# Moving most of one attention into the gaps of a recurrent loop, on one Trainium2 core

## The chip, the core and the metric

The kernel runs on one core of one Trainium2 chip. The metric is device time in microseconds (us), the median over several executions of the same program; lower is better. The names of the engines are those of the profile: PE is the matrix engine, PEld its weight loads (they overlap with PE: in the kernel before PE was busy for 1098.6 us and PEld for 645.9 of a span of 1339.3), DVE the vector engine, ACT the scalar engine (it does the exponentials), POOL the general engine, SP the engine that issues the DMA transfers. "PEclk" is the share of full speed that the profile records as granted to PE; in the records it is 1.0 or 0.5 at any time, and 0.5 is called half clock here.

## The reference

Two attentions read the same `x` (2048 tokens of 512 features), and a gate mixes their results.

```python
def _A_ref(x, mem0, Wq, Wk, Wv, Wo, seg_len):     # 32 heads of 128; seg_len 32
    mem = mem0                                    # 8 memory tokens
    for s in range(64):
        h = concat([mem, x[:, 32*s:32*s+32]])     # 40 tokens
        q, k, v = h @ Wq, h @ Wk, h @ Wv
        p = softmax(mask(q @ k.T * scale))        # causal, memory always seen
        o = (p @ v) @ Wo
        mem = o[:, :8]                            # feeds segment s+1
        outs.append(o[:, 8:])

def _B_ref(x, wq, wk, wv, wo, beta):              # 32 heads of 16
    M = z = 0
    for s in range(4):                            # 4 chunks of 512 tokens
        p = softmax(causal(qs @ ks.T * scale))
        a_mem = (phi(qs) @ M) / (phi(qs) @ z + 1e-6)
        o = g * a_mem + (1 - g) * (p @ vs)        # g = sigmoid(beta)
        M += phi(ks).T @ vs;  z += phi(ks).sum()  # phi(t) = t+1 if t>0 else exp(t)
    return o_all @ wo

g = sigmoid((x * gate_w).sum(-1))
return g * a + (1 - g) * b
```

A is a chain: segment s+1 cannot start before the memory rows of segment s are out of `Wo`. B has no such chain between its 32 heads and, apart from the small `M`, none between its chunks. B is therefore work that may be placed nearly anywhere.

## The kernel before

The kernel is a list of operations per engine, in program order; a helper derives the semaphores. First all of B is done, and its result before `wo` stays on the chip (`oT`). Then comes the loop over the 64 segments of A.

B works on four heads at a time ("g"), and in waves of four 128x128 score blocks. One wave is sixteen matmuls and four exponentials of up to 128x512:

```python
        def f_lg(pe):
            ins = None
            for j in range(4):
                for slot, n in enumerate(wv):
                    qc, kc = blocks[n]
                    ins = pe.matmul(pb[j][:, 128 * slot:128 * (slot + 1)],
                                    KTg[32 * j:32 * j + DH, 128 * kc:128 * kc + 128],
                                    QTg[32 * j:32 * j + DH, 128 * qc:128 * qc + 128],
                                    start=True, stop=True, tile_position=(32 * j, 0))
            return ins
        # ... cut ...
        for j in range(4):
            P.op("act", (lambda j=j: (lambda a: a.activation(
                ptb[:, j, 128 * n0:128 * (n0 + len(wv))], pb[j][:, 0:128 * len(wv)], ACT.Exp, scale=SCALE_B)))(),
                 reads=[rbank[j]], writes=[rpts[j]], name="ex%d_%d_%d_%d" % (sb, g, w, j))
```

A segment of A has 40 tokens at most, of which 32 go through the main path (8 memory rows and 24 tokens; the last 8 tokens of four segments are done together as "left" units). A projection puts 32 rows of tokens into one of four column groups of PE, so that four matmuls with 128x32 weights fill a bank ("column-tiled" below). The order of a segment is written out:

```python
        nat_pass("K", 0, "act")
        nat_pass("K", 1, "dve")
        nat_pass("Q", 0, "act")
        tr("K", 0, "dve")
        nat_pass("Q", 1, "act")
        tr("K", 1, "dve")
        tr("Q", 0, "act")
        nat_pass("V", 0, "dve")
        tr("Q", 1, "act")
        scores(0)
        nat_pass("V", 1, "dve")
        sums(0)
        norm(0)
        scores(1)
        take_fill(2)
        # ... cut: sums(1), pv(0), evictions, norm(1), pv(1), evictions ...
        wo(0)
        take_fill(1)
        wo(1)
        aw = aW_sb
        raw = Rs("aWsb")
        evac("dve", aw[:, :], pb[wb["bk"]][:, 0:128], [wb["bk"]], [raw], "aW%d" % s)
        # ... cut ...
        P.op("pe", lambda pe: pe.transpose(pb16[bk][:, 0:128], aw[:, :], ident[:, :]), reads=[raw, Rs("ident")],
             writes=[rbank[bk]], name="aT%d" % s)
        # ... cut: two copies by DVE, one of them into hT, the input of the next segment ...
```

The output projection uses 128 matmuls of 128 columns for each segment: the column group j of PE computes the output columns 128j to 128j+127, for all heads. One eviction and one transposition then give the memory rows for the next segment (the "carry").

```python
                    for h in range(16 * b + 8 * half, 16 * b + 8 * half + 8):
                        for j in range(4):
                            ins = pe.matmul(pb[bk][SEG * j:SEG * (j + 1), 0:128], OT_sb[:, h, 0:SEG],
                                            Wo_sb[:, h, 128 * j:128 * (j + 1)], start=(h == 0), stop=(h == H - 1))
```

The softmax here doesn't subtract the row's maximum and nothing guards it: scores larger than these inputs give would overflow.

## Time and profile before

The median was 1338.86 us in three runs.

In this document "ahead" is the time from the start of the span to the first K projection of segment 0, and "loop" is the rest. Both come from the profiled execution. In the kernel before, the line is drawn at 352.3 us, though this projection starts at 354.0; by the exact definition its loop is 985.3 us. Busy time counts the time in which at least one instruction of the engine runs. Matmuls overlap in the trace: the 8192 of the output projection below last 221 ns each, which would be 1810 us in sum, and keep PE busy for 142.7 us. Busy time therefore does not say how near PE is to its peak.

| before | ahead | loop |
|---|---|---|
| length, us | 352.3 | 987.0 |
| PE busy, us | 231.9 | 866.7 |
| ACT busy, us | 204.5 | 417.2 |
| mean PEclk | 0.78 | 0.99 |
| time at half clock, us (counted from the clock records of the trace) | 152.6 | 27.9 |

From the page of the kernel before, these are the busy time of PE, and PE's busy tenths and granted clock in 40 equal slices of the span.

```profile
PE 1098.6 (82%) x31189; PEld 645.9 (48%) x31237; DVE 600.9 (45%) x1556; ACT 621.8 (46%) x1408; POOL 173.7 (13%) x399
...
PE   4767667675788888888889888898988888988897
...
PEclk8978787667899999999999999999999999999999
```

The first ten slices (335 us, B) have digits of 4 to 7 with a clock of 0.6 to 0.9; the loop has 8 and 9 with a clock near 1. The same kernel by two stretches, where the columns are the stretch, its length, the busy time and the count of instructions of PE, PEld, DVE, ACT and POOL, then PEclk, the share of the DMA engines and GB/s:

```profile
0.00:352.00 352.00, 231.87 (x4732) 153.63 (x4765) 199.27 (x552) 204.54 (x452) 101.52 (x194) 0.78 0.17 62
352.00:1339.00 987.00, 866.73 (x26460) 492.25 (x26473) 401.65 (x1004) 417.22 (x957) 72.20 (x205) 0.99 0.02 6
```

No engine is full ahead of the loop. In the loop PE is busy for 867 of 987 us, and 120 us of it are gaps. Two groups of the page, B's exponentials and the output projection of A, show the duration of one instruction and what the engine waited for just before it:

```profile
L643 ACT ACTIVATE PT_g<-ps 128x512 bf16<-128x512 f32 (+1 forms) x384 | 170.2, 529 | 60.2 <-PE ps L634 57.8
L1099 PE MATMUL ps<-Wo_sb,OT_sb 128*32 128x128 bf16 x8192 | 142.7, 221 | 29.5 <-issue 29.5
```

This view is of PE's own waits in the loop, with the sum, the number and the longest one in us:

```profile
PE ps L1063 <- DVE Pn_sb L1051: 44.9, 60, 1.4
PE ps L1099 <- issue: 29.5, 28, 1.8
PE ps L941 <- DVE hT L1154: 17.5, 14, 1.3
PE ps L854 <- DVE hT L1154: 5.0, 19, 0.3
```

PE waits 44.9 us for normalised probabilities, 22.5 us for the carry (`hT`), and 29.5 us inside the output projection for nothing that the profile shows ("issue"). One such gap in the order of time, with start and duration in us:

```profile
700.73 0.90 PE L1099 MATMUL ps<-Wo_sb,OT_sb 128*32 128x128 bf16 x52
703.29 0.35 PE L1099 MATMUL ps<-Wo_sb,OT_sb 128*32 128x128 bf16 x12 [1.67 <-issue]
```

The run of 128 matmuls stops after 116 of them, and goes on 1.67 us later.

### The profile page before, as it was taken

To read this page: it belongs to the slowest core of one execution; us is meant where nothing else is said; L and a number is where in the kernel's file an instruction comes from. 1 tells how busy PE (TensorE), PEld (TensorE's weight loads), DVE (VectorE), ACT (ScalarE), POOL (GpSimd) and SP (SyncE) were. 2 spreads that over 40 slices of the span, in tenths; PEclk is the share of its full clock that TensorE was granted. 3 is DMA by queue.
4 is the path that set the end of the run, shared out by engine and by line. 5 is a ranking of instruction groups with operands and counts; after the bars stand their busy time and mean duration, and the time that the engine had idled before them with its cause. 6 is when DMAs were issued, how large, how long until landed. Compare 5 with 4: busy or idle time off the path is not lost.

```text
span 1339.3 us, 67341 instructions
## 1 busy us (share of the span) xinstructions
PE 1098.6 (82%) x31189; PEld 645.9 (48%) x31237; DVE 600.9 (45%) x1556; ACT 621.8 (46%) x1408; POOL 173.7 (13%) x399
## 2 busy tenths in 40 slices
PE   4767667675788888888889888898988888988897
PEld 3444445344344545444544445554554545545454
DVE  3556667655333434344443434433443444434343
ACT  3757646475244444444444344434444444434343
POOL 5322312132000000000000000010000000000000
PEclk8978787667899999999999999999999999999999
DMA  9400000000300000000000000000000000000000
GB/s 357 149 2 3 2 2 2 2 2 2 127 4 3 8 8 4 7 4 7 4 8 4 7 3 8 7 4 8 4 7 4 8 4 7 4 7 7 4 4 11
DMA packets 12864, 27.38 MB, mean 20 GB/s; under 512 B 800, under 2 KB 11048, under 8 KB 11048
## 3 DMA queue, kind: packets, MB, share of 16 engines
q1 hardware_dynamic: 12584, 23.09, 4.7%
q8 instruction: 244, 4.00, 1.2%
q14 instruction: 36, 0.29, 0.1%
HBM read 20.99 MB, written 2.10 MB: 17 GB/s over the span
## 4 chain that ended last, share of the span: by engine, by line
PE 68%; DVE 13%; ACT 10%; issue 7%; DMA 2%; SPq 0%; DVEq 0%; POOL 0%; ACTq 0%
PE ps L854 33%; PE ps L1099 10%; ACT PT_g L643 6%; PE ps L863 6%; PE ps L553 2%; PE ps L1063 2%; PE ps L634 2%; PE ps L1019 2%; DVE Pn_sb L1049 1%; PE ps L1039 1%; PE ps L1072 1%; PE ps L923 1%; DVE QTg L557 1%; PE ps L958 1%; DVE V_sb L846 1%
## 5 line engine op out<-in xcount | busy, mean ns | idle before, releaser
L643 ACT ACTIVATE PT_g<-ps 128x512 bf16<-128x512 f32 (+1 forms) x384 | 170.2, 529 | 60.2 <-PE ps L634 57.8
L1099 PE MATMUL ps<-Wo_sb,OT_sb 128*32 128x128 bf16 x8192 | 142.7, 221 | 29.5 <-issue 29.5
L1099 PEld LDWEIGHTS ps<-Wo_sb,OT_sb 128*32 128x32 bf16 x8192 | 123.1, 97 | 45.0 <-issue 35.2
L1139 POOL COPY OTL<-OT_sb 128x256 bf16<-128x256 bf16 x64 | 25.6, 401 | 895.4 <-DVE OT_sb L846 895.4
L846 DVE CAST V_sb<-ps 128x512 bf16<-128x512 f32 x128 | 88.5, 692 | 110.0 <-PE ps L854 110.0
L854 PE MATMUL ps<-Wk_sb,hT 128*32 128x512 bf16 x2048 | 131.3, 400 | 6.3 <-DVE hT L1154 5.0
L854 PE MATMUL ps<-Wq_sb,hT 128*32 128x512 bf16 x2048 | 135.8, 384 | 0.0
L854 PE MATMUL ps<-Wv_sb,hT 128*32 128x512 bf16 x2048 | 134.8, 381 | 0.0
L844 ACT ACTIVATE QN_sb<-ps 128x512 bf16<-128x512 f32 x128 | 76.4, 597 | 124.4 <-PE ps L854 124.4
L844 ACT ACTIVATE KN_sb<-ps 128x512 bf16<-128x512 f32 x64 | 38.2, 597 | 170.0 <-PE ps L854 170.0
L649 POOL TENSOR_SCALAR_AFFINE_SELECT PT_g<-PT_g 128x512 bf16<-128x512 bf16 x128 | 82.5, 645 | 219.6 <-ACT PT_g L643 217.4
L846 DVE CAST KN_sb<-ps 128x512 bf16<-128x512 f32 x64 | 44.3, 692 | 140.7 <-PE ps L854 140.7
L844 ACT ACTIVATE QT_sb<-ps 128x512 bf16<-128x512 bf16 x128 | 76.4, 597 | 45.4 <-PE ps L863 45.4
L846 DVE COPY KT_sb<-ps 128x512 bf16<-128x512 bf16 x128 | 54.4, 425 | 89.2 <-PE ps L863 89.2
L846 DVE CAST OT_sb<-ps 128x320 bf16<-128x320 f32 x128 | 62.8, 490 | 65.7 <-PE ps L1072 64.5
L634 PE MATMUL ps<-QTg,KTg 16*128 16x128 bf16 x1280 | 43.4, 246 | 52.0 <-ACT PT_g L643 48.8
L854 PEld LDWEIGHTS ps<-Wk_sb,hT 128*32 128x32 bf16 x2048 | 55.0, 100 | 63.7 <-DVE hT L1154 17.4
L844 ACT ACTIVATE OT_sb<-ps 128x320 bf16<-128x320 f32 x128 | 54.8, 428 | 47.2 <-PE ps L1072 47.2
L854 PEld LDWEIGHTS ps<-Wq_sb,hT 128*32 128x32 bf16 x2048 | 51.3, 98 | 49.9 <-issue 5.0
L1063 PE MATMUL ps<-Pn_sb,V_sb 32*128 32x40 bf16 x2048 | 35.6, 177 | 47.3 <-DVE Pn_sb L1051 44.9
L854 PEld LDWEIGHTS ps<-Wv_sb,hT 128*32 128x32 bf16 x2048 | 49.5, 95 | 30.5
L846 DVE CAST aW_sb<-ps 128x128 bf16<-128x128 f32 x64 | 18.7, 292 | 97.7 <-PE ps L1099 97.7
(135 smaller groups left out, 1808.2 us busy)
## 6 DMA issues: line engine op xcount, KB each, us to landing
Wk_sb<-in_A_Wk_dram SPq DMA_DIRECT2D x4, 1024.0 KB, 11.5
Wq_sb<-in_A_Wq_dram SPq DMA_DIRECT2D x4, 1024.0 KB, 20.5
Wo_sb<-in_A_Wo_dram SPq DMA_DIRECT2D x4, 1024.0 KB, 19.7
Wv_sb<-in_A_Wv_dram SPq DMA_DIRECT2D x4, 1024.0 KB, 9.2
x_sb<-in_A_x_dram SPq DMA_DIRECT2D x4, 512.0 KB, 5.7
out_dram<-fin_sb SPq DMA_DIRECT2D x16, 128.0 KB, 1.7
wqN_sb<-in_B_wq_dram SPq DMA_DIRECT2D x1, 512.0 KB, 7.4
wkN_sb<-in_B_wk_dram SPq DMA_DIRECT2D x1, 512.0 KB, 8.4
```

The costliest lines, as they stand in the source:

```text
L553: ins = pe.matmul(pb[7][:, 0:LB], wqB_sb[:, c, g * 128:(g + 1) * 128], xT[:, c, T0p:T0p + LB], start=(c == 0), stop=(c == C - 1))
L634: ins = pe.matmul(pb[j][:, 128 * slot:128 * (slot + 1)], KTg[32 * j:32 * j + DH, 128 * kc:128 * kc + 128], QTg[32 * j:32 * j + DH, 128 * q ...
L643: P.op("act", (lambda j=j: (lambda a: a.activation(ptb[:, j, 128 * n0:128 * (n0 + len(wv))], pb[j][:, 0:128 * len(wv)], ACT.Exp, scale=SCA ...
L649: P.op("gp", (lambda n=n: (lambda gq: gq.affine_select(ptb[:, :, 128 * n:128 * (n + 1)], ptb[:, :, 128 * n:128 * (n + 1)], [[0, 4], [1, 128]],
L844: P.op("act", lambda a: a.activation(dst, src, ACT.Copy), reads=[rbank[k] for k in bks], writes=dres, name=name)
L846: P.op("dve", lambda d: d.tensor_copy(dst, src), reads=[rbank[k] for k in bks], writes=dres, name=name)
L854: ins = pe.matmul(pb[bk][SEG * j:SEG * (j + 1), :], lhs(c), w_sb[:, c, n0:n0 + 512], start=(c == 0), stop=(c == C - 1))
L863: ins = pe.transpose(pb16[bk][:, i * 128:(i + 1) * 128], nat[:, b, i * 128:(i + 1) * 128], ident[:, :])
L1019: ins = pe.matmul(pb[bk][SEG * j:SEG * (j + 1), L * i:L * (i + 1)], KT_sb[:, 4 * b + i, j, :], QT_sb[:, 4 * b + i, j, :], start=False, sto ...
L1063: ins = pe.matmul(pb[bks[j]][:, L * i:L * (i + 1)], V_sb[SEG * j:SEG * (j + 1), b, i * E:(i + 1) * E], Pn_sb[SEG * j:SEG * (j + 1), b, L * ...
L1099: ins = pe.matmul(pb[bk][SEG * j:SEG * (j + 1), 0:128], OT_sb[:, h, 0:SEG], Wo_sb[:, h, 128 * j:128 * (j + 1)], start=(h == 0), stop=(h == ...
L1139: P.op("gp", lambda gq: gq.tensor_copy(OTL[par][:, :, 8 * r:8 * r + 8], OT_sb[:, :, SEG:L]), reads=[Rs("OT%d_%d" % (b, hf)) for b in range ...
```

## The change

The intent is to fill PE's gaps in the loop with B's work. B's projections and its first chunk (40 of 160 small "score steps") stay ahead of the loop; their results go to DRAM. The weights of A take 16 MB on the chip (16 loads of 1024 KB on the page); that they leave no room for B's results was the reckoning. The other 120 steps are units inside the first 51 segments, which load what they need from DRAM. At the same time several other things change: how B is computed, the tiling of the output projection, the carry, the order of units within a segment, and the masks and sums of A's softmax, which become four column-tiled matmuls where they were one with 128x128 weights (1,152 more matmuls in all). The whole diff is 1,700 lines long; this is its core.

A step of B is two to four wide matmuls into two banks and one exponential of 128x1024:

```diff
+    def scores(self):                       # one of 160 steps; 10 steps are one job of 8 heads
+        job, G, k = n // 10, (n // 5) % 2, n % 5
+        self.load(job, "k")                 # from DRAM, if not yet there
+        bks = v.BK.pair()
+        # ... cut: which blocks a step has ...
+                    ins = pe.matmul(v.pb[bks[x]][:, o:o + w], KT[e][r, 128 * kc:128 * (kc + 1)], QT[r, q0:q0 + w],
+                                    start=True, stop=True, tile_position=(r.start, 0))
+        P.op("act", lambda a: a.activation(pt[:, :, :], v.ps[:, bks[0]:bks[1] + 1, :], ACT.Exp, scale=v.SCALE_B), ...)
+        # ... cut: causal masks by POOL; pv(), chain() and finish() follow later ...
```

The projections ahead go through `phi`, whose minimum is taken by POOL between an exponential by ACT and a sum by DVE:

```diff
+    def phi(bk, dst, wres, name):
+        P.op("act", lambda a: a.activation(et[:, :], v.pb[bk], ACT.Exp), ...)
+        P.op("gp", lambda g: g.tensor_scalar(et[:, :], et[:, :], 1.0, None, op0=ALU.min), ...)
+        P.op("dve", lambda d: d.scalar_tensor_tensor(dst, v.pb[bk], 0.0, et[:, :], ALU.max, ALU.add), ...)
```

The output projection has 32 matmuls of 512 columns for a segment. Each column group now sums over a quarter of the heads, so four partial sums have to be added. The carry does this: the bank is evicted as a high half (ACT, bf16) and the rest (DVE), and eight matmuls with a selection matrix add and transpose them.

```diff
-                    for h in range(16 * b + 8 * half, 16 * b + 8 * half + 8):
-                        for j in range(4):
-                            ins = pe.matmul(pb[bk][SEG * j:SEG * (j + 1), 0:128], OT_sb[:, h, 0:SEG],
-                                            Wo_sb[:, h, 128 * j:128 * (j + 1)], start=(h == 0), stop=(h == H - 1))
+                for i in range(4):
+                    for j in range(4):
+                        h = 16 * b + 4 * j + i
+                        ins = pe.matmul(pb[bk][SEG * j:SEG * (j + 1), :], OT_sb[:, h, 0:SEG], Wo_sb[:, h, :],
+                                        start=(b == 0 and i == 0), stop=(b == 1 and i == 3))
+                    # ... cut: for two halves of 256 columns, cs ...
+                    evac("act", aW_sb[:, 0, cs], pb[bk][:, cs], [bk], [Rs("aWh%d" % k)], "hi%d_%d" % (s, k))
+                    P.op("dve", lambda d, cs=cs: d.tensor_tensor(aW_sb[:, 1, cs], pb[bk][:, cs], aW_sb[:, 0, cs], ALU.subtract), ...)
+        def w_t():
+                            # ... cut: loops over the four blocks c of columns and k = high, rest ...
+                            ins = pe.matmul(pb[bk][:, SEG * c:SEG * (c + 1)], aW_sb[:, k, 128 * c:128 * (c + 1)], selL[:, :],
+                                            start=(k == 0), stop=(k == 1))
```

The order of a segment is a list (K, Q, V projections; T transpositions; S scores; M sums; N normalisation; PV; E evictions; W output projection; WT carry; Fc and Ff the left units; bS, bP, bT the units of B), with a table of which engine evicts what:

```diff
+A_ORDER = """
+    K1 K0 Q0 Q1 Fc TK0 TQ0 TK1 Ff bP TQ1 bT Fc S0 bS V0 M0 S1 N0 V1 M1 N1 PV0 Fc E0a E0b PV1 W0 E1a E1b W1 Fc bP bP bS
+    WT bS Ff bT""".split()
+A_ENG = dict(K0="dve", K1="act", Q0="act", Q1="act", V0="dve", V1="dve", TK0="dve", TK1="act",
+             TQ0="act", TQ1="act", E0a="act", E0b="act", E1a="act", E1b="dve", last=1)
+    n_pre = DEV.get("n_pre", 40)
+    n_b0, nseg_b = bat.n, DEV.get("nseg_b", 51)
```

## The prediction

> **What bounds the kernel now.** Two phases. By stretches of time, the attention of B, 0 to 337 us: PE about 70% busy, ACT and DVE 60 to 70%, granted PE clock 0.72 to 0.86 for most of it; no engine is full, they wait for each other (PE for ACT's exponentials 44 us, groups by line). The segment loop of A, 347 to 1339 us, 64 segments of 15.5 us: PE busy 868 of 992 us, granted clock 0.98, ACT 417, DVE 402, POOL 72. So B is bound by handovers and A by PE. In the loop PE idles about 124 us: for normalised probabilities (45 us), inside the Wo matmuls with no visible cause ("issue", 29.5 us), for the carried memory at a segment's end (about 25 us).
>
> **What the change does.** B's projections and first chunk (40 of 160 score steps) stay ahead of the loop; 120 steps go into PE's gaps in the first 51 segments.
>
> *Ahead of the loop.* K, Q, V and phi(K): 60 groups of four 128x512 matmuls, about 1.0 us each at the old clock, 60 us. Score steps: 0.25 us of scores (16 matmuls took 0.43 us) and 0.25 us of PV (40 took 1.23 us), 20 us for 40. Exponentials become 128x1024; from 128x256 (0.30 us) and 128x512 (0.52) I estimate 1.0 us, 40 us of ACT, plus 25 us of phi and evictions. PE about 90 us, ACT 65. To this come loads, projections before the first scores, about 20 us of POOL masks ahead of the first causal mask, and the way through DRAM: first steady steps near 28 us. Estimate 125 us in place of 337: minus 210.
>
> *In the loop.* Added PE: 120 x 0.5 = 60 us, chains and transposes 7, the new carry (eight 32-column matmuls for one transpose) 11. Wo goes from 8192 matmuls of 128 columns to 2048 of 512: the same columns, 1.95 us per segment, so streaming gains little (about 6 us), but most of the 29.5 us of issue gaps should go. PE busy: about 935 us. ACT gains 120 x 1.0 and 64 x 0.7 (high halves), to about 590 us; DVE about 490: neither becomes the limit. The carry's chain lengthens by about 1 us, covered by B's steps in 51 segments, not in 13. New waits: a single-buffered K/Q load between jobs, perhaps 15 us in all. Idle: about 85 us. Loop 1020 us, plus 30.
>
> **Sum.** 125 + 1020 = 1145 us. Of 210 us gained ahead, about 30 are given back in the loop. Range 1090 to 1205. Chances: faster by over 2% 0.96, within 2% 0.02, slower 0.02.
>
> [...]filled gaps should keep the loop at 0.98 or more.
>
> **Signs.** Right: the loop begins at 110 to 145 us; a B-carrying segment takes 15.7 to 16.5 us with PE about 92% busy, one without B 14.8 to 15.5; Wo issue gaps below 10 us; exponentials near 1.0 us. Wrong: ACT's long exponentials stand before evictions and softmax on its queue and PE waits for ACT; PE waits for DMA of K/Q or V; the first phase above 160 us because staging waits for stores behind weight loads.
>
> **What would make it wrong.** PE waits on scratch loads in every job (up to 50 us); the carry not covered; or nearly all idle filled (loop below 980).

The sum of this forecast is 125 us ahead and 1020 us in the loop, 1145 us. That filled gaps keep the clock at 0.98 or more was the expectation (1.00 was measured). The figures in it that name no reading of the trace are estimates. Two of them can be set beside the kernel before: about 1.0 us for a group of four 128x512 matmuls, where 32 such groups kept PE busy for 40.6 us (1.27 us each, L553), and 1.95 us of output projection for a segment, where PE was busy for 142.7 us in 64 segments (2.23 us each, L1099).

## More of the kernel before

The weight loads have waits of their own. L863 is the transposition:

```profile
PEld ps L863 <- issue: 27.3, 64, 0.5
PEld ps L863 <- ACT QT_sb L844: 27.2, 64, 0.4
PEld ps L863 <- DVE KT_sb L846: 27.2, 64, 0.4
```

Three times in every segment the load of the identity waits about 0.42 us.

A transposition uses the identity and full 128x128 weights.

## The result

| | before | after |
|---|---|---|
| median, us (range, 4 runs each) | 1338.16 (1333.25 to 1340.42) | 1160.53 (1155.74 to 1162.27) |
| profiled span, us | 1339.3 | 1153.9 |
| ahead, us | 352.3 | 173.9 |
| loop, us | 987.0 | 980.0 |
| PE busy in the loop, us | 866.7 | 898.8 |
| ACT / DVE / POOL busy in the loop, us | 417 / 402 / 72 | 622 / 434 / 162 |
| half clock ahead / in the loop, us | 152.6 / 27.9 | 64.9 / 9.3 |

The ratio was 0.8671, with a 95% interval of 0.8635 to 0.8708, and the result was correct. Every ratio here is the mean time of one kernel's runs over the mean of the other's runs in the same rounds, so it is not quite the ratio of the medians. Executions over 1.5% slower than the fastest of the same kernel are left out of the means.

The kernel is 13% faster. The whole gain is ahead of the loop: the loop took 120 more steps of B and still became 5 to 7 us shorter. These are the same views of the kernel after; first the page.

```profile
PE 1012.0 (88%) x24359; PEld 559.7 (49%) x24389; DVE 491.1 (43%) x1229; ACT 692.1 (60%) x1427; POOL 248.7 (22%) x573
...
PE   4667769999999999999999999999999998988886
...
PEclk8798779999999999999999999999999998999999
```

PE has digits of 9 from the seventh slice (from 173 us) to the segments that have no work of B left. The two stretches:

```profile
0.00:174.00 174.00, 113.19 (x987) 57.68 (x1005) 57.49 (x111) 69.85 (x95) 86.26 (x178) 0.81 0.56 186
174.00:1154.00 980.00, 898.78 (x23380) 502.01 (x23384) 433.62 (x1118) 622.26 (x1332) 162.42 (x395) 1.00 0.06 16
```

The groups that answer to B's exponentials and to the output projection:

```profile
L734 ACT ACTIVATE PTa<-ps 128x1024 bf16<-128x1024 f32 x147 | 150.4, 1024 | 42.2 <-PE ps L726 40.6
...
L1139 PE MATMUL ps<-Wo_sb,OT_sb 128*32 128x512 bf16 x2048 | 126.2, 381 | 0.1
```

The 529 ns of the kernel before are a mean of two shapes: one exponential of 128x512 lasted 602 ns and one of 128x256 384 ns. They overlap with their neighbours, so that ACT was busy for 0.52 us per exponential of 128x512 (131.9 us for 256). One of 128x1024 lasts 1.02 us and keeps ACT busy for about as long, so the wide form saves little: 160 of them take 164 us, where the 384 before took 170.2. The output projection has almost no gaps (0.1 us). PE's waits in the loop:

```profile
PE ps L1102 <- DVE Pn_sb L1092: 25.4, 62, 0.9
PE ps L1160 <- ACT LN_sb L312: 14.8, 31, 0.9
PE ps L1160 <- ACT VL L312: 4.8, 11, 0.9
PE ps L1160 <- DVE aW_sb L1149: 4.7, 4, 1.4
PE ps L987 <- DMA oTg<-scr_oTd: 3.8, 1, 3.8
```

The wait for probabilities fell from 45 to 25 us. The carry (L1160) costs 24.3 us in three lines; the releasers named there are only those that came last by semaphore. DRAM was waited for once for 3.8 us (for a result of B stored just before), and four times, 1.3 us in all, for `QTa`. The part of a segment that had the gap above, in the order of time:

```profile
502.76 2.24 PE L1139 MATMUL ps<-Wo_sb,OT_sb 128*32 128x512 bf16 x32
...
505.36 0.36 PE L772 MATMUL ps<-Va,PTa 128*128 128x17 bf16 x8
505.65 0.39 PE L726 MATMUL ps<-QTa,KTa 32*128 32x512 bf16 x2
506.36 0.58 PE L1160 MATMUL ps<-selL,aW_sb 128*128 128x32 bf16 x8 [0.32 <-ACT LN_sb L312]
```

The 32 matmuls of the output projection run without a gap, then a unit of the left rows, then PV and scores of B stand where PE would wait for the carry's evictions, and only 0.32 us of waiting are left. Finally the weight loads of the transposition (now L885):

```profile
PEld ps L885 <- issue: 28.7, 72, 0.4
```

One such wait per segment is left of three.

### The profile page after: what moved, and what is told of

Same layout as the page of the kernel before. It is cut to its first block, busy times and chain, and to the rows that moved or that the text cites. A ratio compares the mean times of both kernels' runs of the same rounds, so it can differ in the third digit from the quotient of the medians.

```text
span 1153.9 us, 54295 instructions
## 1 busy us (share of the span) xinstructions
PE 1012.0 (88%) x24359; PEld 559.7 (49%) x24389; DVE 491.1 (43%) x1229; ACT 692.1 (60%) x1427; POOL 248.7 (22%) x573
## 3 DMA queue, kind: packets, MB, share of 16 engines
q8 instruction: 192, 3.15, 1.1%
## 5 line engine op out<-in xcount | busy, mean ns | idle before, releaser
L742 POOL TENSOR_SCALAR_AFFINE_SELECT PTa<-PTa 128x256 bf16<-128x256 bf16 (+1 forms) x205 | 90.1, 440 | 419.1 <-ACT PTa L734 387.6
L734 ACT ACTIVATE PTa<-ps 128x1024 bf16<-128x1024 f32 x147 | 150.4, 1024 | 42.2 <-PE ps L726 40.6
L1139 PE MATMUL ps<-Wo_sb,OT_sb 128*32 128x512 bf16 x2048 | 126.2, 381 | 0.1
L1149 DVE TENSOR_TENSOR aW_sb<-ps,aW_sb 128x256 bf16<-128x256 f32 x128 | 48.4, 420 | 128.1 <-ACT aW_sb L312 126.1
L312 ACT ACTIVATE aW_sb<-ps 128x256 bf16<-128x256 f32 x128 | 42.2, 381 | 92.5 <-PE ps L1139 92.5
L1191 POOL COPY OTL<-OT_sb 128x256 bf16<-128x256 bf16 x64 | 25.4, 397 | 319.4 <-DVE OT_sb L314 319.4
L312 ACT ACTIVATE OT_sb<-ps 128x320 bf16<-128x320 f32 x192 | 75.7, 428 | 24.9 <-PE ps L1111 24.9
L726 PE MATMUL ps<-QTa,KTa 32*128 32x512 bf16 (+1 forms) x448 | 55.6, 305 | 24.4 <-DMA QTa<-scr_qTd 13.1
L314 DVE CAST KN_sb<-ps 128x512 bf16<-128x512 f32 x64 | 44.2, 690 | 75.6 <-PE ps L876 75.6
L314 DVE COPY KT_sb<-ps 128x512 bf16<-128x512 bf16 x64 | 27.2, 425 | 111.0 <-PE ps L885 111.0
L1139 PEld LDWEIGHTS ps<-Wo_sb,OT_sb 128*32 128x32 bf16 x2048 | 46.6, 95 | 49.9 <-ACT OT_sb L312 20.7
L1081 ACT ACTIVATE R_sb<-ps 128x160 f32<-128x160 f32 x128 | 38.8, 303 | 33.7 <-PE ps L1077 33.3
```

Of the source, the lines that this page charges most:

```text
L312: P.op("act", lambda a: a.activation(dst, src, ACT.Copy), reads=[v.rbank[k] for k in bks], writes=dres, name=name)
L314: P.op("dve", lambda d: d.tensor_copy(dst, src), reads=[v.rbank[k] for k in bks], writes=dres, name=name)
L726: ins = pe.matmul(v.pb[bks[x]][:, o:o + w], KT[e][r, 128 * kc:128 * (kc + 1)], QT[r, q0:q0 + w], start=True, stop=True, tile_position=(r.s ...
L734: P.op("act", lambda a: a.activation(pt[:, :, :], v.ps[:, bks[0]:bks[1] + 1, :], ACT.Exp, scale=v.SCALE_B), reads=[v.rbank[b] for b in bks ...
L742: P.op("gp", lambda g, mv=mv: g.affine_select(mv, mv, [[0, mv.shape[1]], [1, 128]], ALU.is_ge, 0.0, base=0, channel_multiplier=-1), reads= ...
L1081: P.op("act", lambda a: a.activation(R_sb[:, b, :], pb[bk][:, 224:384], ACT.Ln), reads=[rbank[bk]], writes=[Rs("R%d" % b)], name="ln%d_%d" ...
```

## The experiments

Twelve kernels were run. The table has what was timed; the text after it says what each tells apart. "Before" is the median of the kernel before in the same rounds; e1 to e4, e5 to e8 and e9 to e12 ran on three different chips, between which it differs by 4 us.

| run | median, us (range) | before, us | ratio [95%] | ahead / loop, us | half clock ahead / loop, us |
|---|---|---|---|---|---|
| after | 1160.53 (1155.74 to 1162.27) | 1338.16 | 0.8671 [0.8635, 0.8708] | 173.9 / 980.0 | 64.9 / 9.3 |
| e1_all_ahead | 1250.67 (1249.24 to 1251.97) | 1336.58 | 0.9342 [0.9300, 0.9384] | 308.9 / 938.6 | 201.4 / 5.1 |
| e2_80_ahead | 1198.22 (1196.02 to 1200.93) | 1336.58 | 0.8945 [0.8896, 0.8994] | 219.5 / 979.6 | 129.7 / 23.5 |
| e3_after_old_wo | 1234.85 (1231.21 to 1243.63) | 1336.58 | 0.9234 [0.9178, 0.9289] | 176.2 / 1058.8 | 64.9 / 77.8 |
| e4_before_new_wo | 1349.87 (1349.35 to 1351.93) | 1336.58 | 1.0086 [1.0041, 1.0131] | 354.1 / 994.1 | 157.0 / 8.5 |
| e5_wo_in_four (3 fast runs) | 1270.06 (1264.92 to 1276.90) | 1339.61 | 0.9488 [0.9438, 0.9537] | 177.0 / 1098.0 | 75.1 / 92.3 |
| e6_ahead_old_order | 1327.00 (1324.10 to 1329.05) | 1339.61 | 0.9907 [0.9878, 0.9936] | 312.4 / 1014.8 | 221.9 / 14.3 |
| e7_exp_twice | 1246.97 (1245.07 to 1248.17) | 1339.61 | 0.9310 [0.9284, 0.9335] | 179.0 / 1067.1 | 81.9 / 44.2 |
| e8_scores_twice | 1182.19 (1180.35 to 1183.69) | 1339.61 | 0.8828 [0.8799, 0.8858] | 175.8 / 1003.7 | 64.9 / 15.9 |
| e9_after_again | 1159.65 (1155.53 to 1160.97) | 1340.43 | 0.8644 [0.8606, 0.8681] | 174.6 / 980 | 64.9 / 9.3 |
| e10_min_on_dve | 1131.47 (1128.15 to 1135.44) | 1340.43 | 0.8441 [0.8400, 0.8481] | 151.6 / 980.5 | 44.4 / 9.9 |
| e11_plus_loads (wrong result) | 1167.60 | 1340.43 | 0.8695 [0.8655, 0.8735] | 149.9 / 1016 | not used |
| e12_30_ahead (wrong result) | 1204.26 | 1340.43 | 0.8981 [0.8943, 0.9019] | 136.1 / 1065 | not used |

My theory was that B's steps are cheap in the loop because they fill gaps of PE. The rivals were that the gain comes from the rewriting of B (wide exponentials), from the new output projection, or from the new order of units, and that the place of the steps matters little. Runs e1, e2 and e6 separate these; e3, e4 and e5 test the output projection; e7 and e8 test which engine pays for a step; e9 to e12 test the part ahead of the loop.

### All steps ahead: e1_all_ahead

```diff
-    n_pre = DEV.get("n_pre", 40)
+    n_pre = DEV.get("n_pre", 160)
```

> The changed kernel with all 160 score steps ahead of the loop, none in it. Theory 'gaps' (a step costs little inside the loop because PE waits there anyway): the loop falls by only about 40 us (51 segments x 0.66 us plus one 5 us wait), to about 940 us, while 120 steps ahead cost about 1.3 us each (one 1.02 us exponential on ACT and what it waits for), 156 us; total about 1275 us. Rival 'rewritten B' (the gain is the wide exponentials and full-width projections, wherever they stand): total 1190 us or less.

It took 1250.67 us, between the 1275 that I had expected and the 1190 of the rival. The placement of 120 steps is worth 90 us (1250.67 - 1160.53). Ahead grew by 135.0 us, 1.13 us for a step (expected 1.3); the loop shrank by 41.4 us, 0.35 us for a step (about 40 us expected). The stretches of this run show why a step is dear ahead. The first line below is the time in which it does only steps, the second one is its loop:

```profile
174.00:309.00 135.00, 109.95 (x1360) 53.69 (x1364) 52.76 (x166) 100.59 (x104) 79.62 (x167) 0.52 0.21 55
309.00:1247.50 938.50, 821.31 (x21892) 454.44 (x21896) 385.11 (x938) 505.29 (x1212) 71.51 (x203) 1.00 0.03 8
```

In the first of them ACT is busy for 100.6 of 135 us, so each step waits for its exponential of 1.02 us and for the handovers around it, and PE runs at a clock of 0.52. In the loop the clock is 1.00, and a step cost 0.35 us.

How far is "it fills gaps" true? The loop with the steps has 898.8 us of busy PE, the one without has 821.3; so 120 steps add 77.5 us of work, 36 us of which came out of idle time (117 to 81), and 41 us lengthen the loop. About half of a step is hidden in a gap. Which gap this is can be read from the waits of e1 in its loop:

```profile
PE ps L1160 <- ACT LN_sb L312: 42.3, 45, 1.1
...
PE ps L1160 <- ACT VL L312: 14.1, 15, 0.9
...
PE ps L1160 <- DVE aW_sb L1149: 5.5, 4, 1.4
```

The carry costs 61.9 us here, and 24.3 us in the kernel after. The difference, 37.6 us, is the whole of the idle time that the steps filled. The wait for probabilities hardly changed (23.6 and 25.4 us).

### Half of the steps ahead: e2_80_ahead

```diff
-    n_pre = DEV.get("n_pre", 40)
+    n_pre = DEV.get("n_pre", 80)
```

> The changed kernel with 80 of 160 steps ahead of the loop instead of 40. Theory 'gaps': 40 steps x 1.3 us more ahead, about 13 us less in the loop: about 1200 us. Rival 'rewritten B': within 10 us of 1160 us. If the loop were overfull with 2.35 steps a segment, this would be the faster of the two.

Ahead took 219.5 us, 45.6 us more for 40 steps (1.14 us for each, as in e1). The loop should have been 14 us shorter than in the kernel after (a third of 41.4 us); it was the same, 979.6 us. Two segments of 25.1 and 23.8 us, where others take about 15, stand for most of this: PE waits there for a tile of B's result that had just been stored to DRAM (9.4 us in 2 waits) and then runs at half clock (23.5 us in this loop against 9.3). How many steps fall into each segment decides where such a job ends, and nothing in the program keeps it away from the unit that reads the result. The total of 1198 us agrees with the 1200 that I had expected, but partly by luck: ahead grew by less than the expected 52 us, and the loop did not shrink by 13.

### The old order of units: e6_ahead_old_order

This is e1 with the order of the kernel before written as a list, and its engines.

```diff
-    n_pre = DEV.get("n_pre", 40)
+    n_pre = DEV.get("n_pre", 160)
 A_ORDER = """
-    K1 K0 Q0 Q1 Fc TK0 TQ0 TK1 Ff bP TQ1 bT Fc S0 bS V0 M0 S1 N0 V1 M1 N1 PV0 Fc E0a E0b PV1 W0 E1a E1b W1 Fc bP bP bS
-    WT bS Ff bT""".split()
-A_ENG = dict(K0="dve", K1="act", Q0="act", Q1="act", V0="dve", V1="dve", TK0="dve", TK1="act",
-             TQ0="act", TQ1="act", E0a="act", E0b="act", E1a="act", E1b="dve", last=1)
+    K0 K1 Q0 TK0 Q1 TK1 TQ0 V0 TQ1 S0 V1 M0 N0 S1 Fc Ff M1 PV0 E0b N1 E0a Fc PV1 E1a E1b W0 Fc W1 Fc WT Ff""".split()
+A_ENG = dict(K0="act", K1="dve", Q0="act", Q1="act", V0="dve", V1="dve", TK0="dve", TK1="dve",
+             TQ0="act", TQ1="act", E0a="act", E0b="dve", E1a="dve", E1b="act", last=1)
```

> As the run with all 160 steps ahead (1250.7 us, loop 938.5 us), but the units of a segment in the old sequence and on the old engines. Theory 'the order list itself pays': the loop with the new Wo in the kernel before took 994 us, so the loop goes back by 40 to 55 us, total 1290 to 1305 us. Rival 'the order only matters for hosting B's steps': 1245 to 1260 us.

It took 1327.00 us, 1% less than the kernel before and more than the 1290 to 1305 that I had expected. So the rewritten B, the new output projection and the new sums and masks together, in the old place and the old order, are worth about 12 us. Ahead fell from 352 to 312 us, and the loop grew from 987 to 1015 us. The order and the engines are worth 76 us beside this kernel (1327.00 to 1250.67), all of it in the loop (1014.8 to 938.6), with the same PE instructions:

```profile
312.40:1327.20 1014.80, 862.68 (x21892) 443.27 (x21900) 432.85 (x1067) 459.94 (x1084) 72.01 (x203) 0.99 0.03 7
```

PE is busy for 862.7 us here and for 821.3 us in e1, although both run 21,892 matmuls. The weight loads show what changed. In e6 the transposition (here L884) waits three times a segment, as in the kernel before:

```profile
PEld ps L884 <- issue: 28.0, 64, 0.8
PEld ps L884 <- DVE KT_sb L314: 27.2, 64, 0.4
PEld ps L884 <- ACT QT_sb L312: 27.2, 64, 0.4
```

In e1 one is left:

```profile
PEld ps L885 <- issue: 27.2, 64, 0.4
```

In these loops the load of full 128x128 weights for a transposition behind column-tiled matmuls waited 0.42 us (27.2 us in 64 waits), once for each group of transpositions: 82.4 us in sum with three groups, 27.2 us with one, so 55 us less. PE's waits for probabilities fell from 38.8 to 23.6 us as well, and a wait of 17.4 us for the exponentials of A is gone from the list. These can overlap, so they are not an exact sum. Of the 76 us, 35 are idle time of PE (152.1 us here, 117.2 in e1), for which the waits for probabilities and exponentials are nearly enough. The other 41 us are busy time, and that the weight loads explain them is a reading: the list and the table were changed as a whole, and grouping was not run by itself.

The 76 us also depend on what else has changed. Run e4 below has the new output projection in the kernel before, with the old order and the old sums and masks, and its loop took 994.1 us, 20.7 us less than this one; its PE waited 1.0 us for the exponentials of A, and here it waited 17.4. Beside e4's loop the one of e1 is 55.5 us shorter. The column-tiled sums and masks, and the rule by which left units are taken, are among the differences between e4 and e6 in the loop; no run separates them.

### The new output projection: e3_after_old_wo, e4_before_new_wo, e5_wo_in_four

e3 is the kernel after with the old output projection and the old carry.

```diff
-                        ins = pe.matmul(pb[bk][SEG * j:SEG * (j + 1), :], OT_sb[:, h, 0:SEG], Wo_sb[:, h, :], ...)
+                            ins = pe.matmul(pb[bk][SEG * j:SEG * (j + 1), 0:128], OT_sb[:, h, 0:SEG],
+                                            Wo_sb[:, h, 128 * j:128 * (j + 1)], start=(h == 0), stop=(h == H - 1))
# ... cut: the loops as before; one eviction by DVE and one transposition for the carry ...
```

> The changed kernel with the old output projection (8192 matmuls of 128 columns) and the old carry (one 128x128 eviction, one transpose). Theory 'the new Wo removes issue gaps in PE': PE idle without a visible cause comes back inside these matmuls, about 29 us, the shorter carry gives back about 5 us: total 1180 to 1190 us. Rival 'Wo is neutral, only its column count matters': 1155 to 1165 us. Rival 'the short carry is better': below 1150 us.

It took 1234.85 us, 74 us more than the kernel after, where I had expected 20 to 30 us. The loop is 79 us longer. The first line of PE's waits is again "issue", in the output projection:

```profile
PE ps L1138 <- issue: 52.8, 41, 2.2
```

That is more than the 29.5 us of the kernel before, and the loop had 77.8 us at half clock, where the kernel after had 9.3.

e4 is the opposite: the kernel before with the new output projection and its carry. To make room for the larger carry tile, the tile `t1` is bf16 in it.

```diff
-                            ins = pe.matmul(pb[bk][SEG * j:SEG * (j + 1), 0:128], OT_sb[:, h, 0:SEG],
-                                            Wo_sb[:, h, 128 * j:128 * (j + 1)], start=(h == 0), stop=(h == H - 1))
+                        ins = pe.matmul(pb[bk][SEG * j:SEG * (j + 1), :], OT_sb[:, h, 0:SEG], Wo_sb[:, h, :], ...)
# ... cut: high half by ACT, rest by DVE, eight matmuls with selL ...
-    t1_sb = sbt("t1_sb", [128, DM], F32, esA)
+    t1_sb = sbt("t1_sb", [128, DM], BF16, esA)
-DEV = dict(do_b=True, nseg_limit=None)
+DEV = dict(do_b=True, nseg_limit=None, psum_rr=True)    # keeps readers of one bank in order
```

> The kernel before with only the new output projection and carry (2048 matmuls of 512 columns, high and low halves, eight summing matmuls)[...]; one scratch row is kept in bf16 to make room. Theory: the issue gaps (29.5 us) go, but with nothing to put into the longer carry PE waits about 0.5 to 0.8 us more in each of 64 segments, 30 to 50 us: total 1340 to 1365 us, so the new Wo pays only together with B's steps. Rival 'the new Wo is worth its issue gaps by itself': 1305 to 1315 us.

It took 1349.87 us, 0.9% more than the kernel before. The issue gaps in the output projection are gone, as predicted, and 62 us of waits for the longer carry stand in their place:

```profile
PE ps L1161 <- DVE aW_sb L1110: 48.9, 50, 1.4
...
PE ps L1161 <- ACT LN_sb L844: 13.2, 14, 0.9
```

So the new output projection is no gain by itself in the old order. With the new order and B's steps it is worth 74 us (e3). I read this as the steps filling the longer carry: its waits are 62 us here, 61.9 in e1 and 24.3 in the kernel after. It isn't shown that the steps alone make the difference: the old output projection in the new order without steps was not run.

e3 changed the tiling and the carry together. e5 leaves everything as in the kernel after, and only splits each matmul of 512 columns into four of 128.

```diff
-                        ins = pe.matmul(pb[bk][SEG * j:SEG * (j + 1), :], OT_sb[:, h, 0:SEG], Wo_sb[:, h, :],
-                                        start=(b == 0 and i == 0), stop=(b == 1 and i == 3))
+                        for c in range(4):
+                            ins = pe.matmul(pb[bk][SEG * j:SEG * (j + 1), 128 * c:128 * (c + 1)], OT_sb[:, h, 0:SEG],
+                                            Wo_sb[:, h, 128 * c:128 * (c + 1)],
+                                            start=(b == 0 and i == 0 and c == 0), stop=(b == 1 and i == 3), skip_group_check=True)
```

> The changed kernel with each output-projection matmul of 512 columns cut into four of 128: the same layout, sums, carry and columns, but 8192 matmuls and weight loads again instead of 2048. Theory 'instruction supply': the number of PE instructions alone brings the gaps without a visible cause back (41 gaps, 53 us in these matmuls in the run with the old Wo)[...]; total 1215 to 1250 us, with 40 or more us of such gaps and over 50 us of half clock in the loop. Rival 'the old carry or the old layout made the old Wo slow': 1155 to 1170 us.

In its three fast runs it took 1270.06 us, 110 us more than the kernel after, for the same columns, the same sums and the same carry. That is more than the 1215 to 1250 that I had expected. PE's waits in its loop:

```profile
PE ps L1140 <- issue: 54.0, 38, 2.2
...
PE ps L876 <- issue: 4.4, 4, 1.2
PE ps L944 <- issue: 4.3, 3, 1.6
PE ps L772 <- issue: 3.9, 4, 1.2
```

The idle time of PE rose by 65 us (81 to 147), and these four lines sum to 66.6 us (the largest waits that are new against the kernel after). The other 53 us are busy time: the same work at a clock of 0.96, with 92.3 us at half clock in place of 9.3. By the recorded 0.5, I estimate half of the additional 83 us as lost to the clock, 42 us, and the rest I put down to the cost of more instructions. So it is the number of PE instructions (matmuls, each with its weight load), and neither the layout nor the carry, that brings the gaps. The profile does not name what PE waits for in them. The instruction queue moved 192 packets (3.15 MB) in the kernel after, 236 in e3, 240 in e5 and 244 (4.00 MB) in the kernel before, 16 KB each. In the loop of e3 all 45 "issue" gaps of over 0.5 us end 1.19 to 1.57 us after the end of such a packet (median 1.40), although the packets are 4.4 us apart; in e5 the 48 gaps end 1.19 to 1.60 us after one, and in the kernel before the 24 gaps 1.27 to 1.53 us. PE's gaps of that length with another releaser show no such interval (0.4 to 3.8 us in e3). I read the gaps as waits for instructions, but this stays an inference; no run here changed the supply alone.

The half clock after such gaps deserves a word. In the four traces that I checked (before, after, e3 and e5), every half-clock stretch but the last one of each trace lasted 3.413 us or a whole multiple of it. Most of the gaps were 1 to 2.2 us long, within stretches of busy PE, and the loop of e3 had 21 half-clock stretches against 2 in the kernel after (in each, one of them at the end of the program). If the loops are cut into windows of 3.413 us, in step with the clock records, the traces say more: each of the 20 others of e3 follows a window in which PE was idle for 1.1 to 2.9 us in sum. In all four loops every full-clock window with more than about 1.9 us of idle time was followed by half clock and none with less than about 1.1 us was; between the two, both happened. In the kernel before, the seven windows that half clock followed had 1.34 to 2.02 us of idle time and the others at most 1.63; in the kernel after it was one window of 2.17 us, and the others had at most 1.53. By what rule the clock is set was not shown.

### Which engine pays for a step: e7_exp_twice, e8_scores_twice

e7 does the exponential of each step in the loop twice.

```diff
-        P.op("act", lambda a: a.activation(pt[:, :, :], v.ps[:, bks[0]:bks[1] + 1, :], ACT.Exp, scale=v.SCALE_B), ...)
+        for _ in range(2 if n >= self.n_pre else 1):
+            P.op("act", lambda a: a.activation(pt[:, :, :], v.ps[:, bks[0]:bks[1] + 1, :], ACT.Exp, scale=v.SCALE_B), ...)
```

> The changed kernel with the exponential of each of the 120 steps in the loop done twice (the same result): 123 us more of ACT in the loop, 622 to about 745 of 980 us, nothing more for PE. Theory 'the loop pays for PE work, ACT has room': less than 30 us longer, up to 1190 us. Rival 'the long exponentials hold up evictions and softmax on ACT's queue': 60 us or more longer.

It took 1246.97 us, 86 us more, for 123 us of added ACT time (120 times 1.024 us). So my theory (less than 30 us) was wrong here, and the rival (60 us or more) was right. ACT was busy for only 622 of 980 us in the loop, 64%, and yet 70% of the added time showed up. PE's largest wait became this one, which was not in the list of the kernel after:

```profile
PE ps L1078 <- ACT P_sb L1061: 38.6, 50, 1.0
```

The sums of A's softmax wait for A's own exponential, which stands behind B's on ACT's queue. One exponential of 1.02 us fits behind the V projection that stands at this place (1.05 us); a second one does not. The share of busy time of ACT said nothing about this; the place in the order did. The kernel after is therefore not limited by ACT, but it is at the edge there.

e8 doubles the score matmuls of the steps in the loop instead.

```diff
-            for e, kc, q0, w, o in mms:
+            for e, kc, q0, w, o in mms * (2 if n >= self.n_pre else 1):
```

> The changed kernel with the score matmuls of each of the 120 steps in the loop done twice (the same result): about 0.25 us more of PE per step, 30 us, nothing more for the other engines. Theory 'PE is the limit where the steps stand': 20 to 30 us longer, 1180 to 1190 us. Rival 'the steps stand in waits and are free': 5 us or less.

It took 1182.19 us, 22 us more. PE was busy for 31 us longer (0.26 us for a step's scores, as the prediction had it: 0.25), and 24 us of that lengthened the loop. PE time was mostly paid in full in this loop (24 of 31 us); the kernel after has 81.2 us of idle PE left in 980.

### The stretch ahead: e9_after_again, e10_min_on_dve, e11_plus_loads, e12_30_ahead

The prediction had 125 us for this stretch, and it took 173.9. The groups of instructions ahead of the loop in the kernel after have the chain of `phi`: the exponential by ACT (L564), the minimum by POOL (L565) and the sum by DVE (L566).

```profile
L565 POOL TENSOR_SCALAR etmp<-etmp 128x512 bf16<-128x512 bf16 x24 | 35.6, 1483 | 23.1 <-ACT etmp L564 21.7 <-POOL PTa L742 0.6 <-POOL etmp L565 0.6
...
L564 ACT ACTIVATE etmp<-ps 128x512 bf16<-128x512 f32 x24 | 14.4, 598 | 28.8 <-DVE stgq L314 21.8 <-PE ps L599 2.4 <-POOL PTa L742 2.3
...
L566 DVE SCALAR_TENSOR_TENSOR phK<-ps,etmp 128x512 bf16<-128x512 f32 x12 | 8.3, 692 | 18.2 <-POOL etmp L565 14.1 <-PE ps L599 2.4 <-issue 1.6
L566 DVE SCALAR_TENSOR_TENSOR stgp<-ps,etmp 128x512 bf16<-128x512 f32 x12 | 8.3, 692 | 27.7 <-POOL etmp L565 18.6 <-ACT stgk L312 4.6 <-ACT PTa L734 2.3
```

The minimum takes 1.48 us on POOL, 24 times, and DVE waits 14.1 and 18.6 us for it. PE's largest waits in this stretch are for the first load of Q and then for `phi`:

```profile
PE ps L726 <- DMA QTa<-scr_qTd: 11.8, 1, 11.8
PE ps L619 <- DVE phK L566: 8.1, 3, 3.3
...
PE ps L726 <- DVE stgp L566: 4.9, 3, 2.2
```

e9 is the kernel after once more, unchanged, on the chip and in the rounds of e10 to e12, as their base.

> The changed kernel again, as the control for the three that follow on the same chip: 1150 to 1170 us.

It took 1159.65 us, which agrees with 1160.53 us before.

e10 moves the minimum to DVE.

```diff
-        P.op("gp", lambda g: g.tensor_scalar(et[:, :], et[:, :], 1.0, None, op0=ALU.min), reads=[re], writes=[re], name=name + "_m")
+        P.op("dve", lambda d: d.tensor_scalar(et[:, :], et[:, :], 1.0, None, op0=ALU.min), reads=[re], writes=[re], name=name + "_m")
```

> The changed kernel with the 24 minimum steps of phi on DVE instead of POOL (1.48 us each on POOL; a minimum of the same size took 0.37 us on DVE in the kernel before). Theory 'the stretch ahead of the loop is a chain of handovers, and POOL's 1.48 us stand in it': the loop begins 8 to 15 us earlier, total 8 to 15 us below the control. Rival 'PE and the stores set the pace there': within 4 us of the control.

It took 1131.47 us, 28 us less than e9 in the same rounds, more than the 8 to 15 that I had expected. It is the fastest correct version, 15.6% below the kernel before by the ratio. The minimum takes 0.30 us on DVE:

```profile
L565 DVE TENSOR_SCALAR etmp<-etmp 128x512 bf16<-128x512 bf16 x24 | 7.2, 300 | 13.0 <-ACT etmp L564 13.0
```

Ahead fell by 23.0 us (174.6 to 151.6): PE's idle time there by 16 us, and its busy time by 7 us (114.4 to 107.1), with 20.5 us less at half clock (64.9 to 44.4). The time that POOL saves is 28 us (24 times 1.18 us). The loss of PE's clock fell with it, so this chain had cost more than PE's waits. The loops of the two profiled executions are equal (980 and 980.5 us), and these two differ by 22.6 us; the 28 us are the difference of the medians. The same instruction took 1483 ns on POOL and 300 ns on DVE, 4.9 times as long on POOL.

e11 tries, on top of e10, to bring the first scores forward: the second job's loads after the third step, the weights of A held back until ten pieces of projection are planned, and the steps spread over 50 segments. e12 is e11 with 30 steps ahead.

```diff
     for part in "kv":
-        for job in range(2):
-            bat.load(job, part)
+        bat.load(0, part)
     for n in range(n_pre):
         bat.scores()
+        if n == 2:
+            for part in "kv":
+                bat.load(1, part)
-        if weights and done % 3 == 0:
+        if weights and done >= 10 and done % 3 == 0:
-    n_b0, nseg_b = bat.n, DEV.get("nseg_b", 51)
+    n_b0, nseg_b = bat.n, DEV.get("nseg_b", 50)
```

> As the run with the minimum on DVE, and also: A's weights are held back until the first K and Q of B are on their way, the second job's loads are issued after the third step, and B ends one segment earlier (50 instead of 51 segments). Theory 'the first scores wait for the queue' (PE waited 11.8 us for the first Q, and 3.8 us for the last stored tile at the end of B): 5 to 12 us less than the run with the minimum on DVE alone. Rival 'the loads only land later somewhere else': within 3 us of it.

> As the run before it, with 30 instead of 40 score steps ahead, 2.6 a segment in the loop. A step took 1.13 us ahead and 0.35 to 0.5 us in the loop: 6 to 8 us less than the run before it. Rival 'the loop is full at 2.35 a segment': no gain, or a loss of up to 10 us.

Both gave a wrong result on the chip, with relative errors of 0.0418 and 0.0415. This was not intended. Their times, 1167.60 and 1204.26 us, are therefore not evidence for a version that computes the reference. What can be read from them is only that their loops were longer, about 1016 and 1065 us, with waits of PE for loads from DRAM (27.5 us in the listed lines of e11), so the schedule of the steps decides how well loads are covered.

The likely cause of the wrong result was found by reading the code, and the traces bear it out. In the loop the tile with V, phi(Q) and M of a job has a single buffer. The load for the next job is planned when its first PV is planned. If this happens before the previous job's last chain is planned, the load stands in front of that chain in program order, and the chain, which was to read the old phi(Q) and M, is ordered behind the load and reads the new ones. This is a consistent order for a dependency tracker, so no race is to be found. Whether it happens depends on how many steps fall into which segment; 120 and 80 steps over 51 segments, and none in the loop, all gave correct results. The traces show the order of the loads of M (`MZa`) and of the two chains of a job that read it. In the kernel after and in e2 each load comes behind both chains of the job before; in e11 it stands between the two chains at two changes of job, and in e12 at three. So the order is shown, and that it makes the whole error is not. What the earlier loads and the held-back weights are worth stays open.

## Why the prediction was right, and where it was not

The prediction was 1145 us with a range of 1090 to 1205, and 1160.5 was measured. The total was right, in part by luck: the two terms of its sum each missed, by 49 and 40 us, in opposite directions.

| term | predicted, us | measured, us | run that shows why |
|---|---|---|---|
| ahead | 125 | 173.9 | e10 |
| PE busy in the loop | 935 | 898.8 | e6 against e1 |
| PE idle in the loop | 85 | 81.2 | e1 |
| loop | 1020 | 980.0 | |
| sum | 1145 | 1153.9 (span), 1160.5 (median) | |

**Ahead: "Estimate 125 us in place of 337" was 49 us too low.** The sum had PE's and ACT's work (90 and 65 us), the loads and POOL's masks. ACT measured 69.9 us, which is right. PE measured 113.2 us, 23 more than predicted; 64.9 us of the stretch were at half clock (PEclk 0.81), which I estimate, at half of that time, at up to 32 us. The term that was missing altogether is the minimum of `phi` on POOL, 1.48 us in a chain of three engines; e10 shows that it cost 23 us of this stretch. The first scores began at 30.8 us, near the predicted 28. Another 27 us (151.6 - 125) are left in e10 with 44.4 us at half clock; their cause was not isolated. The sign that I had given for "the first phase above 160 us", that staging waits for stores behind weight loads, came true as to the time (173.9 us) and had the wrong cause: no wait for a store is among PE's largest waits there, and `phi` is.

**The loop: "PE busy: about 935 us" was 36 us too high.** I took the order list as neutral. The terms of the prediction sum to 872 us without the steps (867 + 11 - 6) and 67 us for the steps, 939 in all, which it rounded to 935. The runs give 862.7 us without the steps in the old order (e6), 41.4 us less by the new order (e1, 821.3), and 77.5 us for the steps (898.8). So the steps cost 10 us more than predicted, the base was 9 us smaller, and the order, which the prediction did not have, took off 41. The lines that could have told me were in the profile before: three waits of 0.42 us in each segment before transpositions.

**Idle: 85 us predicted, 81.2 measured.** "The carry's chain lengthens by about 1 us, covered by B's steps in 51 segments" is confirmed by e4 (62 us of waits where nothing covers it), e1 (61.9) and the kernel after (24.3).

**"Most of the 29.5 us of issue gaps should go"** is right: 0.1 us are left. But the gain from it was undervalued for this kernel. With the small matmuls, the loop with B's steps would not have had 29.5 us of gaps but 53 to 54, and 77.8 and 92.3 us at half clock besides (e3, e5): 74 and 110 us of time.

**"A single-buffered K/Q load between jobs, perhaps 15 us in all"** was 5.1 us (3.8 for `oTg` and 1.3 for `QTa`). In this trace the loads of a job landed after medians of 1.9 to 2.7 us, and they were issued early enough. e2 shows that a different spread of the steps brings such waits back (9.4 us, and segments of 25 us).

**Segments.** One with B's steps took 15.26 us in the mean (predicted 15.7 to 16.5), one without 14.5 us (14.8 to 15.5), if the one of 21.0 us is left out that waits 3.8 us for B's last stored result, and PE was busy for 92% of the loop (898.8 of 980.0), as predicted. Where a B-carrying segment was expected to be longer than a segment of the kernel before (15.36 us), it is equally long: in e1, with the new order and no steps, a segment took 14.55 us. ACT was busy for 622 us of the loop (predicted about 590) and DVE for 434 (about 490); neither became the limit, though e7 shows that ACT is close to it.

**The causes of the gain, in order.** With the medians, 1338 to 1327 us is the rewritten B, output projection, sums and masks in the old place and order (e6), 1327 to 1251 us is the order and the choice of engines (e1), and 1251 to 1161 us is the move of 120 steps into the loop. This is one path through the parts; since parts depend on each other (e4), another path would give other shares.

## What to carry to other kernels

Work without dependences was cheap here where the busiest engine waits for a chain, and dear where it stands alone: a step of B cost 1.13 us ahead of the loop and 0.35 us in it. Before changing what is computed, count the places where the tile shape of the matrix engine changes (the weight load of a transposition waited 0.42 us at each, 82.4 us in e6 with three in a segment and 27.2 us in e1 with one), and the number of its instructions; in e5 the same columns in four times as many matmuls cost 110 us. The share of busy time did not say whether ACT had room (it was busy for 622 of 980 us, and 86 of the 123 us that e7 added showed up); ask what stands behind the added instruction on its queue.
